# Wide mask matmuls ahead of the scores, and three early loads split by partitions, in an attention and SwiGLU kernel

## The chip, the cores and the metric

One core of one Trainium2 chip. The metric is the device time of the whole kernel in microseconds (us), lower is better. In traces, PE is TensorE, PEld its weight load, DVE VectorE, ACT ScalarE, POOL GpSimd, SP the engine that issues the DMAs.

## The reference

```python
def _attn_ref(q, k, v):                      # [8, 8, 576, 64], float32
    scores = q @ k.T / 8                     # per batch and head
    rel = pos[:, None] - pos[None, :]
    scores = where((rel >= 0) & (rel < 64), scores, -1e9)
    return softmax(scores) @ v
def _moe_ref(x, w_gate, w_val, w_out):       # x: [4608, 512], d_ff 1536
    g = x @ w_gate
    return (g * sigmoid(g) * (x @ w_val)) @ w_out
```

A causal sliding window of 64 keys, then a gated feed-forward block.

## The kernel before

Tokens go in 36 groups of 128. Queries, keys and values are loaded in float32, cast to bf16, turned by TensorE, and each group's scores, weights and products are worked between feed-forward steps. The first groups are masked in PSUM, by adding -1e30 through a matmul of a constant (`minus`) with the identity; later groups are masked after the exponential by VectorE. The parts that the change touches:

```python
    def load_vg(g):

        if g % 2 == 0:
            staged["v_f", g // 2] = stage.tile([P, 2, H, D], FP32, name="v_f", tag="v_f")[:]
        for y, b, s in tokens(g):
            m = y.stop - y.start
            sp.dma_start(
                staged["v_f", g // 2][y, g % 2],
                v[b, :, s:s + m, :].rearrange("h r d -> r h d"))
...
    def scores(g, masked=False):

        ps = [ps_a.tile([P, 4, 2, 64], FP32, name="s_ps", tag="a") for _ in range(2)]
        for b in range(2):
            o = P * (g % 2) + 64 * b
            for p in range(4):
                for a in range(2):
                    y = slice(64 * a, 64 * a + 64)
                    keys = kT[g // 2 % KR][y, p, o:o + P]
                    if ORDER[g][1] is None:
                        keys = kL[y, p, ORDER[g][0] + b, :]
                    nc.tensor.matmul(
                        ps[a][:, p, b], keys, qT[g // 2 % QR][y, p, o:o + 64],
                        tile_position=(64 * a, 0), start=True, stop=not masked,
                    )
                if masked:
                    for a in range(2):
                        y = slice(64 * a, 64 * a + 64)
                        m = minus[1 if ORDER[g][1] == 0 and b == 0 else 0]
                        nc.tensor.matmul(
                            ps[a][:, p, b], m[y], identb[y, y], tile_position=(64 * a, 0),
                            start=False, stop=True,
                        )
        sps[g] = ps, masked
...
    def weights(s, i):
        src = (moe_w_gate, moe_w_val)[i]
        w_f = wst.tile([P, 4, 256], FP32, name="w_f", tag="w_f")
        sp.dma_start(w_f[:], src[:, 256 * s:256 * s + 256].rearrange("(c r) f -> r c f", r=P))
        raw[i, s] = w_f
```

The schedule is written by hand; its start, in the order in which each engine gets its work (`warm(n)` is n matmuls on zeros whose result nothing uses):

```python
    begin()
    load(0, k, "k_f")
    load(0, q, "q_f")
    load(1, k, "k_f")
    load_vg(0)
    cast_k(0, "q_f", (dve, act))
    cast_k(0, "k_f", pool)
    warm(11)
    turn2(0, "k_f", (act, dve))
    load(1, q, "q_f")
    warm(3)
    turn2(0, "q_f", (act, dve))
    warm(3)
    scores(0, True)
    scores(1)
    load_vg(1)
    cast_k(1, "k_f", (act, dve))
    cast_v(0, (pool, act, dve))
    load_vg(2)
    load_vg(3)
    cast_v(1, pool)
    weigh(1)
    weights(5, 0)
    weigh(0)
    warm(7)
    turn2(1, "k_f", act)
...
```

Here `scores(0, True)` is a masked group; seven groups are (0, 2, 3, 5, 4, 7, 6). `weights(5, 0)` is the first slice of the gate weights: 128 rows of 4 pieces of 1 KB.

The softmax here doesn't subtract the row's maximum and nothing guards it: scores larger than these inputs give would overflow.

## Time and profile before

| | before |
|---|---|
| time, median | 338.14 us (337.61 to 338.68) |
| TensorE busy | 327.6 us, 97% |
| TensorE idle, 8 to 39 us of the span | 4.3 us |
| TensorE idle, 39 to 332 us | none |
| matmuls and weight loads on TensorE | 2825 + 2825 = 5650 (the prediction counts 5652) |

Two stages: up to about 38 us the DMA engines are full (share 1.06 from 8 to 40 us) and TensorE waits for data now and then; after that TensorE never waits. One thing is needed to follow the rest: each load of 128 rows in this kernel, and each of the later ones of 64 rows, leaves 16 landing records in the trace. They are read here as one from each of the core's 16 DMA engines, though no record names its engine, and a load is taken as there when the last one is. Landings below are read from these records; where a view shows them indirectly, it is as the start of the cast that waits for the load.

### The profile page before, as it was taken

Reading aid. Unit: us, or ns where it says so; the run is one execution under the profiler, and the core shown is the slowest. Engines: PE = TensorE matmul, PEld = TensorE weight load, DVE = VectorE, ACT = ScalarE, POOL = GpSimd, SP = SyncE. Lnnn points to the kernel's source line nnn. Section 1 sums busy time; section 2 is a strip of 40 time slices with the busy share of each in tenths; the row PEclk is TensorE's granted clock in tenths of the full one; section 3 lists DMA queues with packets and bytes.
Section 4 is the critical chain, followed back from the end, with each engine's and each line's share of the span. In section 5 each row is a group of like instructions: output and inputs, shape, how many; then the busy total and the mean of one; then the engine's idle time right before and its main releaser. Section 6 shows DMA issues by size and latency. Waiting matters only on the chain.

```text
span 336.9 us, 7388 instructions
## 1 busy us (share of the span) xinstructions
PE 327.6 (97%) x2825; PEld 164.1 (49%) x2825; DVE 226.3 (67%) x491; ACT 151.9 (45%) x268; POOL 100.5 (30%) x148
## 2 busy tenths in 40 slices
PE   7898999999999999999999999999999999999996
PEld 3555665555544444444444444444444444444444
DVE  4657889895676666666676767766667766655520
ACT  3766876664634343434343443434343434233222
POOL 4444356660053333333333333223333200000000
DMA  8999999998978999798879798999787720211013
GB/s 209 247 312 264 280 301 326 322 185 194 228 137 149 192 151 190 151 193 162 181 151 194 137 195 174 158 179 181 158 180 157 104 62 34 65 31 31 33 47 109
DMA packets 150612, 56.85 MB, mean 169 GB/s; under 512 B 124721, under 2 KB 144561, under 8 KB 150577
## 3 DMA queue, kind: packets, MB, share of 16 engines
q1 hardware_dynamic: 150576, 56.38, 77.5%
q8 instruction: 22, 0.36, 0.5%
q14 instruction: 14, 0.11, 0.2%
HBM read 37.75 MB, written 9.44 MB: 140 GB/s over the span
## 4 chain that ended last, share of the span: by engine, by line
PE 87%; DMA 8%; SPq 3%; ACT 1%; POOL 0%; issue 0%; ACTq 0%; POOLq 0%
PE g_ps L309 27%; PE o_ps L327 27%; PE v_ps L309 26%; DMA q_f<-in_q_dram 6%; PE ao_ps L245 3%; PE s_ps L207 3%; DMA v_f<-in_v_dram 2%; SPq L110 1%; SPq L89 1%; PE tp L170 1%; DMA out_dram<-os__4994 1%; PE xtp L269 0%; POOL q_fb L120 0%; ACT q_fb L118 0%; ACT os__4994 L332 0%
## 5 line engine op out<-in xcount | busy, mean ns | idle before, releaser
L309 PE MATMUL g_ps<-xT,wg 128*128 128x512 bf16 (+1 forms) x460 | 112.4, 367 | 0.2
L309 PE MATMUL v_ps<-xT,wv 128*128 128x512 bf16 (+1 forms) x460 | 112.1, 366 | 0.5 <-ACT wv L118 0.5
L320 DVE SCALAR_TENSOR_TENSOR sg<-th,g_ps 128x512 f32<-128x512 f32 (+1 forms) x115 | 75.0, 652 | 53.8 <-ACT th L314 53.5
L314 ACT ACTIVATE th<-g_ps 128x512 f32<-128x512 f32 (+1 forms) x115 | 65.9, 573 | 76.4 <-PE g_ps L309 73.6
L327 PE MATMUL o_ps<-wo,hT 128*128 128x512 bf16 (+2 forms) x456 | 98.5, 368 | 0.0
L321 DVE TENSOR_TENSOR hT<-sg,v_ps 128x512 bf16<-128x512 f32 (+1 forms) x115 | 75.4, 656 | 11.9 <-PE xtp L269 0.5
L309 PEld LDWEIGHTS <-wv 128*128 128x128 bf16 x460 | 44.7, 98 | 49.4 <-ACT wv L118 1.0
L327 PEld LDWEIGHTS <-hT 128*128 128x128 bf16 x456 | 43.6, 98 | 49.5
L309 PEld LDWEIGHTS <-wg 128*128 128x128 bf16 x460 | 41.8, 98 | 42.3 <-issue 0.6
L227 ACT ACTIVATE E<-s_ps 128x512 bf16<-128x512 f32 x72 | 38.5, 596 | 8.0 <-PE s_ps L207 8.0
L120 POOL CAST q_fb<-q_f 128x1024 bf16<-128x1024 f32 x13 | 13.6, 1044 | 64.9 <-DMA q_f<-in_q_dram 41.2
L120 POOL CAST k_fb<-k_f 128x1024 bf16<-128x1024 f32 (+1 forms) x16 | 16.0, 1003 | 56.1 <-DMA k_f<-in_k_dram 46.1
L256 DVE TENSOR_TENSOR x_b<-ao_ps,r 128x256 bf16<-128x256 f32 x72 | 30.6, 425 | 2.5
L120 POOL CAST ve<-v_f 64x512 bf16<-64x512 f32 x47 | 28.9, 615 | 2.9
L229 DVE TENSOR_TENSOR E<-E,mask 128x512 bf16<-128x512 bf16 x58 | 23.3, 427 | 9.1 <-ACT E L227 8.3
L120 POOL CAST vo<-v_f 128x512 bf16<-128x512 f32 x30 | 18.9, 630 | 30.3 <-DMA v_f<-in_v_dram 30.1
L255 DVE RECIPROCAL r<-ao_ps 128x4 f32<-128x4 f32 x72 | 12.6, 174 | 5.4 <-PE ao_ps L245 5.3
L245 PEld LDWEIGHTS <-E 128*64 128x64 bf16 x576 | 11.0, 110 | 7.8 <-issue 5.7
L207 PEld LDWEIGHTS <-kT 64*128 64x128 bf16 x512 | 10.1, 95 | 6.6 <-issue 4.0
L120 POOL CAST vL<-v_f 64x512 bf16<-64x512 f32 x15 | 9.6, 638 | 10.2 <-DMA v_f<-in_v_dram 9.5
L207 PE MATMUL s_ps<-qT,kT 64*128 64x64 bf16 x512 | 12.2, 191 | 0.4 <-DVE x_b L256 0.3
L245 PE MATMUL ao_ps<-ve,E 128*64 128x65 bf16 x256 | 11.9, 196 | 0.1
(100 smaller groups left out, 150.1 us busy)
## 6 DMA issues: line engine op xcount, KB each, us to landing
v_f<-in_v_dram SPq DMA_DIRECT2D x32, 256.0 KB, 4.6
k_f<-in_k_dram SPq DMA_DIRECT2D x20, 256.0 KB, 4.1
q_f<-in_q_dram SPq DMA_DIRECT2D x18, 256.0 KB, 4.7
q_f<-in_q_dram SPq DMA_DIRECT2D x7, 512.0 KB, 7.0
k_f<-in_k_dram SPq DMA_DIRECT2D x6, 512.0 KB, 7.6
w_f<-in_moe_w_gate_dram SPq DMA_DIRECT2D x6, 512.0 KB, 6.2
w_f<-in_moe_w_val_dram SPq DMA_DIRECT2D x6, 512.0 KB, 6.5
wo_f<-in_moe_w_out_dram SPq DMA_DIRECT2D x6, 512.0 KB, 7.3
```

Source lines behind the costliest of these rows:

```text
L120: eng.tensor_copy(y, x)
L207: nc.tensor.matmul(ps[a][:, p, b], keys, qT[g // 2 % QR][y, p, o:o + 64], tile_position=(64 * a, 0), start=True, stop=not masked,)
L227: act.activation(e, x[:], AF.Exp, scale=0.125)
L229: dve.tensor_mul(e, e, mk[:].unsqueeze(1).to_broadcast([P, 4, 2, 64]))
L245: nc.tensor.matmul(o_ps[64 * b:64 * b + 64, i, :], Es[g % ER][:, y, b], z[:, y, :], tile_position=(0, 64 * b),)
L255: dve.reciprocal(r[:], o_ps[:, :, D])
L256: dve.tensor_mul(xb[g][:, 256 * h:256 * h + 256].rearrange("r (y d) -> r y d", y=4), o_ps[:, :, 0:D], r[:].unsqueeze(2).to_broadcast([P, 4 ...
L309: nc.tensor.matmul(ps[:, 0:n], w[:, c, P * m:P * m + P], xT[t][:, c, c0:c0 + n], start=(c == 0), stop=(c == 3),)
L314: act.activation(th[:, 0:n], g_ps[:, 0:n], AF.Tanh, scale=0.5)
L320: dve.scalar_tensor_tensor(sg[:, 0:n], th[:, 0:n], 1.0, g_ps[:, 0:n], ALU.add, ALU.mult)
L321: dve.tensor_mul(hT[t][:, m, c0:c0 + n], sg[:, 0:n], v_ps[:, 0:n])
L327: nc.tensor.matmul(o_ps[:, a:b], hT[t][:, c, P * s:P * s + P], wo[:, c, a:b], start=(c == 0), stop=(c == 11),)
```

## The change

Intent: (1) mask a whole PSUM tile by one wide matmul per row half, ahead of the scores, in place of one narrow matmul after each score: 18 mask matmuls in place of 112. (2) Split three early loads by partitions, so that some DMA engines get less of them.

```diff
--- before.py
+++ after.py
@@ -101,15 +101,17 @@
                 sp.dma_start(x_f[y, i], src[b, :, s:s + m, :].rearrange("h r d -> r h d"))
         staged[nm, n] = x_f[:]
 
-    def load_vg(g):
+    def load_vg(g, cut=P):
 
         if g % 2 == 0:
             staged["v_f", g // 2] = stage.tile([P, 2, H, D], FP32, name="v_f", tag="v_f")[:]
         for y, b, s in tokens(g):
             m = y.stop - y.start
-            sp.dma_start(
-                staged["v_f", g // 2][y, g % 2],
-                v[b, :, s:s + m, :].rearrange("h r d -> r h d"))
+            for i, j in ((0, min(m, cut)), (cut, m)):
+                if i < j:
+                    sp.dma_start(
+                        staged["v_f", g // 2][y.start + i:y.start + j, g % 2],
+                        v[b, :, s + i:s + j, :].rearrange("h r d -> r h d"))
 
     words = {}
 
@@ -196,6 +198,20 @@
     def scores(g, masked=False):
 
         ps = [ps_a.tile([P, 4, 2, 64], FP32, name="s_ps", tag="a") for _ in range(2)]
+        if masked:
+
+            first = ORDER[g][1] == 0
+            for b in range(2 if first else 1):
+                for a in range(2):
+                    y = slice(64 * a, 64 * a + 64)
+                    z, n = ps[a][:].rearrange("r p b x -> r (p b) x"), 8
+                    if first:
+                        z, n = ps[a][:, :, b], 4
+                    nc.tensor.matmul(
+                        z, minus[1 if first and b == 0 else 0][y],
+                        identb[y, y].unsqueeze(1).to_broadcast([64, n, 64]),
+                        tile_position=(64 * a, 0), start=(b == 0), stop=False,
+                    )
         for b in range(2):
             o = P * (g % 2) + 64 * b
             for p in range(4):
@@ -206,16 +222,9 @@
                         keys = kL[y, p, ORDER[g][0] + b, :]
                     nc.tensor.matmul(
                         ps[a][:, p, b], keys, qT[g // 2 % QR][y, p, o:o + 64],
-                        tile_position=(64 * a, 0), start=True, stop=not masked,
+                        tile_position=(64 * a, 0), start=not masked,
+                        stop=not masked or (b == 1 and p == 3),
                     )
-                if masked:
-                    for a in range(2):
-                        y = slice(64 * a, 64 * a + 64)
-                        m = minus[1 if ORDER[g][1] == 0 and b == 0 else 0]
-                        nc.tensor.matmul(
-                            ps[a][:, p, b], m[y], identb[y, y], tile_position=(64 * a, 0),
-                            start=False, stop=True,
-                        )
         sps[g] = ps, masked
 
     def weigh(g):
@@ -278,10 +287,13 @@
 
     raw = {}
 
-    def weights(s, i):
+    def weights(s, i, cut=P):
         src = (moe_w_gate, moe_w_val)[i]
         w_f = wst.tile([P, 4, 256], FP32, name="w_f", tag="w_f")
-        sp.dma_start(w_f[:], src[:, 256 * s:256 * s + 256].rearrange("(c r) f -> r c f", r=P))
+        x = src[:, 256 * s:256 * s + 256].rearrange("(c r) f -> r c f", r=P)
+        for y in (slice(0, cut), slice(cut, P)):
+            if y.start < y.stop:
+                sp.dma_start(w_f[y], x[y])
         raw[i, s] = w_f
 
     def cast_w(s, i, eng):
@@ -394,11 +406,11 @@
     load_vg(1)
     cast_k(1, "k_f", (act, dve))
     cast_v(0, (pool, act, dve))
-    load_vg(2)
-    load_vg(3)
+    load_vg(2, 120)
+    load_vg(3, 104)
     cast_v(1, pool)
     weigh(1)
-    weights(5, 0)
+    weights(5, 0, 100)
     weigh(0)
     warm(7)
     turn2(1, "k_f", act)
```

## The prediction

> **What bounds the kernel now.** I read the page's busy shares first, then the slices, then the chain that ended last in order of time, then the waits of TensorE, and last the DMA records around the loads that the change touches.
>
> ```profile
> PE 327.6 (97%) x2825; PEld 164.1 (49%) x2825; DVE 226.3 (67%) x491; ACT 151.9 (45%) x268; POOL 100.5 (30%) x148
> ...
> PE   7898999999999999999999999999999999999996
> ...
> DMA  8999999998978999798879798999787720211013
> ```
>
> TensorE (PE) is busy 97% of the span; the only slices short of 9 are the first few. DMA is at 8 or 9 tenths over the same start. So there are two stages. Asked for busy time by stage (columns: stretch, its length, busy us and count by engine, clock, DMA share, GB/s), the trace says so sharply:
>
> ```profile
> 8.00:40.00 32.00, 27.70 (x455) 17.45 (x455) 22.60 (x57) 23.69 (x44) 14.19 (x19) 1.00 1.06 273
> 40.00:76.00 36.00, 36.00 (x394) 20.61 (x387) 32.71 (x71) 24.55 (x43) 21.11 (x28) 1.00 1.08 284
> 76.00:320.00 244.00, 244.00 (x1875) 116.00 (x1874) 166.09 (x344) 97.27 (x172) 61.07 (x86) 1.00 0.73 143
> ```
>
> From 40 us on TensorE is busy 36.00 of 36.00 and 244.00 of 244.00 us: whatever is to be won there must be matmul time itself. From 8 to 40 us it idles 4.3 us, and the DMA engines are full (share 1.06; over 1 because packets of one engine overlap). The chain that ended last, in order of time (start, length, what), tells which transfers carry the start:
>
> ```profile
> 9.61 6.56 DMA v_f<-in_v_dram
> ...
> 16.52 10.66 DMA q_f<-in_q_dram
> ...
> 28.16 8.91 DMA q_f<-in_q_dram
> ...
> 37.20 1.05 POOL q_fb L120
> 38.25 0.04 issue
> 38.30 0.62 PE tp L170 x8
> 38.91 0.44 PE g_ps L309 x4
> ```
>
> Three loads, then a cast, then the transposes at 38.30; after that only TensorE to 331.90 and the last store. The end is therefore (the moment at which the queries of block 3 are turned, about 38.3) plus 293.6 us of dense TensorE work plus some 5 us. TensorE's own waits between 10 and 39 us:
>
> ```profile
> PE tp L170 <- DVE q_fb L120: 1.0, 1, 1.0
> PE tp L170 <- ACT q_fb L118: 0.9, 1, 0.9
> PE xtp L269 <- ACT E L227: 0.6, 1, 0.6
> PE v_ps L309 <- ACT wv L118: 0.5, 1, 0.5
> PE tp L170 <- DVE k_fb L120: 0.4, 1, 0.4
> PE s_ps L207 <- DVE x_b L256: 0.3, 1, 0.3
> PE tp L170 <- POOL k_fb L120: 0.2, 1, 0.2
> ```
>
> They sum to 3.9 us; the idle time of the trace from 8 to 39 us is 4.3 us. That is the ceiling of anything that only brings data sooner.
>
> Two more records matter. The masks:
>
> ```profile
> L215 PE MATMUL s_ps<-identb,minus x112: 188/190/200, 8.6 to 40.6; 64*128 64x64 bf16 x112
> ```
>
> [...] in the timeline the pairs (two row halves) start 0.03 us apart. And a 16 KB instruction fetch runs on the DMA engines just when the loads in question are in flight, as the DMA view of 11.5 to 13.5 us shows (packets, MB, share):
>
> ```profile
> q8 instruction: 1, 0.02, 4.1%
> ```
>
> Its packet starts at 11.97 us and takes 1.31 us; the next such fetches are at 21.98 and 33.19 us, and one of 8 KB is at 28.54 us (1.32 us). [...] The load of values 2, issued at 8.38 us, has 15 landings by 13.9 us and the last at 15.2; values 3, issued at 9.61, has 15 by 14.9 and the last at 16.2; the first weight slice 16.9 and 17.6. After the fetch at 21.98 the keys of block 2 land 23.9 and 25.4, their queries 25.7 and 27.2. After those at 28.54 and 33.19 the queries of block 3 have 14 landings by 35.6 and the last two at 36.8 and 37.1. So one DMA engine, held up by a fetch, delays each following load by 1.2 to 1.5 us, and the sequencer that issues (its queue full all through this stage) waits with it.
>
> [...] 4 matmuls of 512 columns take 0.86 us, pairs of 64 columns start 29 ns apart. [...] two halves together take those 29 ns. [...]
>
> **The change part by part.** (1) Masks. Seven score groups are masked (0, 2, 3, 5, 4, 7, 6). Removed: 7 x 16 = 112 matmuls of 64 columns with as many weight loads. Added: 2 groups that start a sequence x 4 of 256 columns, and 5 x 2 of 512: 18 matmuls. Cost before, per group: 8 pairs x 29 ns = 0.232 us. After: one pair of 512, 0.216 us, or two pairs of 256, 2 x 0.109 = 0.218 us. The columns are the same; [...] about 0.015 us a group, 0.1 us in all. Only groups 7 and 6 (39.7 to 40.7 us) lie in the dense stage: 0.03 us of certain gain. (2) The instruction stream of TensorE is shorter by 2 x 94 = 188 (5652 to 5464), 24 less in group 0 and 28 in each of 2, 3, 5. Over the run 22 fetches for some 5652 instructions is about 257 each, so 188 is three quarters of a fetch, all in the first 41 us. By counting, the first fetch moves from 11.97 to about 13.2 us (24 instructions on), the second from 21.98 to about 28 (80 on, as TensorE waits there), the third from 33.2 to about 36. The keys and queries of block 2 would then not meet the second fetch. (3) The splits. Values 2: 120 rows on 15 engines and 8 on 8; values 3: 104 on 13 and 24 on 12; the weight slice: 100 on 10 and 28 on 14. [...] A 256 B packet takes 18 ns and a 1 KB one 46 ns in the trace, so a value row is 8 x 18 = 0.15 us and a weight row 4 x 46 = 0.18: [...] plus 0.45 + 0.74 = 1.2 us for the most loaded. If the engine of the fetch is the last one, values 2 land at about 13.9 + 0.15 = 14.1 in place of 15.2, values 3 at about 15.2 in place of 16.2. ScalarE casts them 1 us sooner, and its exponentials of groups 2 and 3 follow, worth most of the 0.6 us wait of the transposes and part of the 0.3. The weight slice stays near 17.6: 12 rows in place of 8 on ten engines. Three more issues of some 0.5 us (the shortest in the trace) fall in a queue that is full anyway, so they are hidden.
>
> The sum: 0.5 us in the waits to 18 us; the keys and queries of block 2 at max(23.9 + 1.2, no straggler) = 25.1 and 26.9 by load alone, up to 1 us better as the queue no longer stalls on one engine, so 0.4 to 1.0 of the 1.5 us of waits at 26 to 28; the last wait of 0.6 us before 38.3 partly, as the second late engine at 36.8 may remain. These add to 0.9 to 1.9 us of the 4.3; [...] I take 1.2 us.
>
> **Rivals.** (a) Nothing: [...] the straggler becomes later by up to 1.2 us and every load of the start with it; the time is 338.5 to 339.5. For it: no record names the engine. [...] (b) The start gains, but TensorE is held at 38.3 by the queries of block 3, whose arrival is bandwidth, not lag: bytes are unchanged and the load is now uneven. Then the gain is under 0.4 us, 337.8. For it: DMA share 1.06 in that stage. (c) The wide masks run their halves one after the other, as no 512-column pair exists before: 0.216 more in each group, of which two are on the path, +0.4 us. Against it: the 64-column pairs overlap fully. (d) All waits of the start melt: minus 3 us, 335. It needs every load sooner, and the 0.95 us at 11.7 is upstream of the change.
>
> **Range and chances.** 338.14 - 1.2 = 336.9. The two runs before differ by 1.07 us, so half a microsecond is noise; with (a) and (c) above and (d) below, 335.5 to 338.5 should hold it 8 times in 10. Two per cent is 6.8 us, more than all idle time from 8 us on, so faster by that is at 0.01; slower by that would need the whole start to slip by 6.8 us: 0.01; within, 0.98.
>
> **What would show it.** Right: landings of values 2 and 3 near 14 and 15 us; ScalarE's casts of them about 1 us earlier; instruction fetches later by the counts above and one fewer; the wait of the transposes on the query cast near 27 us shorter; TensorE without idle time after some 37 us; the two masked groups near 40 us still some 0.9 us together. Wrong: the last landing of the three loads no sooner, the queries of block 3 still at 37 us, or wide masks whose halves start 0.2 us apart.

The sum came to 0.9 to 1.9 us: 0.5 in the waits to 18 us, 0.4 to 1.0 around block 2, and up to 0.4 left for the last wait of 0.6. Its author took 1.2 of it, 338.14 - 1.2 = 336.9, after a deduction. The "last one" of the engines was assumed to get nothing of the cut parts. The "most loaded" one was taken to get three value rows (0.45) and four weight rows (0.74) more. The number of engines of each part is borne out by the trace of the changed kernel: parts of 120, 8, 104, 24, 100 and 28 rows leave 15, 8, 13, 12, 10 and 14 landings. The 0.109 us of a 256-column matmul and the 0.216 of a 512-column one are the distances of their starts in the trace before. The queue that issues is full in that the issues from 0.8 to 39 us follow each other with gaps of at most 0.2 us. That the scores add to a mask put in first rests on the results, which were correct.

## The result, and the profile after

The changed kernel takes 340.37 us (340.16 to 340.57) where 335.5 to 338.5 was predicted: 2.2 us slower where 1.2 us of gain was expected. All outputs are right. The ratio is 1.0070, 95% interval 1.0046 to 1.0093. A ratio here is the mean time of one kernel's fast runs over that of the other's fast runs of the same rounds, so it is not quite the ratio of the medians quoted beside it. Later, with more rounds, the same kernel gave 1.0041 (1.0013 to 1.0068).

The page of the changed kernel (busy totals; TensorE's busy tenths in 40 slices), to be held against the first fence of the prediction:

```profile
PE 328.0 (97%) x2731; PEld 163.9 (48%) x2731; DVE 226.7 (67%) x491; ACT 151.9 (45%) x268; POOL 101.2 (30%) x148
...
PE   7877999999999999999999999999999999999996
```

TensorE's busy total is 0.4 us more, and the loss is in the first slices. The stretches show the same (same columns as in the prediction):

```profile
8.00:40.00 32.00, 26.17 (x362) 15.98 (x360) 21.05 (x56) 22.75 (x42) 13.07 (x17) 1.00 1.08 255
40.00:76.00 36.00, 36.00 (x381) 20.99 (x380) 32.16 (x71) 25.49 (x45) 20.71 (x27) 1.00 1.13 296
```

From 8 to 40 us TensorE is busy 26.17 us in place of 27.70, so it idles 1.5 us more; from 40 to 76 us it is full as before. Its waits between 10 and 39 us:

```profile
PE tp L172 <- ACT q_fb L120: 1.6, 1, 1.6
PE g_ps L321 <- POOL wg L122: 1.1, 1, 1.1
PE tp L172 <- DVE q_fb L122: 1.0, 1, 1.0
PE v_ps L321 <- POOL wv L122: 0.6, 1, 0.6
PE g_ps L321 <- DVE sg L332: 0.5, 1, 0.5
PE xtp L278 <- ACT E L236: 0.5, 1, 0.5
```

New are the waits for GpSimd's casts of weights (`wg` 1.1, `wv` 0.6) and for VectorE's `sg` that follows; the wait for the queries of block 2 (ScalarE, `q_fb`) grew from 0.9 to 1.6. The wait of the transposes for the exponentials (`xtp`) shrank only from 0.6 to 0.5. The chain that ended last (start, length, what):

```profile
11.73 4.74 DMA v_f<-in_v_dram
...
18.51 11.10 DMA q_f<-in_q_dram
...
29.63 0.63 ACT q_fb L120
...
40.19 0.45 PE tp L172 x8
```

The queries of block 3 are turned at 40.19 us by this view, where before it was 38.30. That is the result in one line. By the start times of TensorE's matmuls in the trace the turn starts 1.72 us later (40.02 against 38.30), the stretch from there to the first output projection takes 34.34 us against 34.38, and the last part 261.66 against 261.16: 1.72 - 0.04 + 0.50 = 2.18 us, the difference of the two ends of TensorE's work (336.02 and 333.84). Of the 1.72 us, 0.44 stand in this profile ahead of anything that the change touches: TensorE's first wait for keys ends at 6.57 us in place of 6.12, and the wait for the queries of block 1 at 13.09 in place of 12.65. In the repeat of the change told below the latter ends at 12.64 us and the turn is at 39.71, so some 1.4 us of the lateness at the turn go with the change.

What came late are the weight slices. GpSimd's casts of the first three, before (start, length, operation, idle before and what ended it):

```profile
17.65 1.04 POOL L120 CAST wg<-w_f 128x1024 bf16<-128x1024 f32 x1 [0.28 <-DMA w_f<-in_moe_w_gate_dram]
19.18 1.04 POOL L120 CAST wv<-w_f 128x1024 bf16<-128x1024 f32 x1 [0.49 <-DMA w_f<-in_moe_w_val_dram]
20.75 1.04 POOL L120 CAST wg<-w_f 128x1024 bf16<-128x1024 f32 x1 [0.52 <-DMA w_f<-in_moe_w_gate_dram]
```

and after:

```profile
20.94 1.04 POOL L122 CAST wg<-w_f 128x1024 bf16<-128x1024 f32 x1 [3.42 <-DMA w_f<-in_moe_w_gate_dram]
22.15 1.04 POOL L122 CAST wv<-w_f 128x1024 bf16<-128x1024 f32 x1 [0.17 <-DMA w_f<-in_moe_w_val_dram]
23.65 1.04 POOL L122 CAST wg<-w_f 128x1024 bf16<-128x1024 f32 x1 [0.46 <-DMA w_f<-in_moe_w_gate_dram]
```

The first slice is cast 3.3 us later and the next two 3.0 and 2.9 us later. In landings: the first slice is complete at 20.8 us in place of 17.6.

### The profile page after: what moved, and what is told of

It is laid out like the page before. It is cut to its first block, busy times and chain, and to the rows that moved or that the text cites. A ratio compares the mean times of both kernels' runs of the same rounds, so it can differ in the third digit from the quotient of the medians.

```text
span 338.9 us, 7208 instructions
## 1 busy us (share of the span) xinstructions
PE 328.0 (97%) x2731; PEld 163.9 (48%) x2731; DVE 226.7 (67%) x491; ACT 151.9 (45%) x268; POOL 101.2 (30%) x148
## 4 chain that ended last, share of the span: by engine, by line
PE 84%; DMA 6%; SPq 4%; ACT 2%; DVE 2%; issue 1%; ACTq 0%; DVEq 0%
PE g_ps L321 26%; PE o_ps L339 26%; PE v_ps L321 25%; DMA q_f<-in_q_dram 3%; PE ao_ps L254 3%; PE s_ps L223 2%; SPq L112 2%; DMA v_f<-in_v_dram 1%; SPq L89 1%; PE tp L172 1%; DMA kT<-k_fb 1%; ACT E L236 1%; DMA out_dram<-os__4903 1%; DVE sg L332 1%; PE xtp L278 1%
## 5 line engine op out<-in xcount | busy, mean ns | idle before, releaser
L238 DVE TENSOR_TENSOR E<-E,mask 128x512 bf16<-128x512 bf16 x58 | 24.6, 452 | 9.3 <-ACT E L236 8.7
L352 PE MATMUL w_ps<-wz 128*128 128x512 bf16 x33 | 10.8, 464 | 1.3 <-DVE wz L356 1.3
L254 PE MATMUL ao_ps<-vo,E 128*64 128x65 bf16 x256 | 11.9, 196 | 0.0
```

Source lines behind the costliest of these rows:

```text
L238: dve.tensor_mul(e, e, mk[:].unsqueeze(1).to_broadcast([P, 4, 2, 64]))
L254: nc.tensor.matmul(o_ps[64 * b:64 * b + 64, i, :], Es[g % ER][:, y, b], z[:, y, :], tile_position=(0, 64 * b),)
L352: nc.tensor.matmul(w_ps[:], wz[:, 0:P], wz[:])
```

## The experiments

Each kernel ran with a profile and five timed rounds beside the kernel before. The times are medians of six runs; the kernel before had a median of 338.6 to 338.7 in every job; the jobs ran on three chips.

| kernel | time, us | ratio to before | 95% interval |
|---|---|---|---|
| the change again | 339.95 | 1.0041 | 1.0013 to 1.0068 |
| masks alone | 337.68 | 0.9977 | 0.9959 to 0.9996 |
| all splits alone | 339.84 | 1.0038 | 1.0017 to 1.0059 |
| slice split alone | 339.20 | 1.0022 | 1.0000 to 1.0043 |
| all three split at 64 | 338.88 | 1.0018 | 0.9995 to 1.0041 |
| masks + slice split | 339.11 | 1.0018 | 0.9998 to 1.0038 |
| masks + value splits | 338.61 | 0.9998 | 0.9980 to 1.0015 |
| wide masks in group 0 only | 337.39 | 0.9967 | 0.9949 to 0.9985 |
| wide masks but group 0 | 339.58 | 1.0041 | 1.0008 to 1.0074 |
| masks + slice at 96 | 338.66 | 1.0001 | 0.9973 to 1.0029 |
| masks + slice at 120 | 339.21 | 1.0021 | 0.9995 to 1.0048 |
| masks + slice by chunks | 337.60 | 0.9972 | 0.9947 to 0.9996 |
| masks + slice in halves | 338.84 | 1.0010 | 0.9985 to 1.0036 |
| masks + slice odd/even | 337.97 | 0.9985 | 0.9960 to 1.0009 |
| group 0 wide, padded | 338.06 | 0.9987 | 0.9955 to 1.0019 |

### Which part: masks alone, splits alone

Edit for the masks alone (against the change):

```diff
-    load_vg(2, 120)
-    load_vg(3, 104)
+    load_vg(2)
+    load_vg(3)
-    weights(5, 0, 100)
+    weights(5, 0)
```

For the splits alone, `scores` is the function before.

> The wide masks as in the change, no load split. Theory A (uneven rows: ten DMA engines get 12 rows of the weight slice in place of 8, so everything behind it lands late): no part of the loss is here; within 0.5 us of before, at best 1 us faster, as the second instruction fetch moves away from the keys and queries of block 2. Rival B (the shorter TensorE stream moves a fetch, seen at 16.0 us in place of 12.0, onto worse loads): 1 to 2 us slower than before, with a straggler in the landings of the weight slices.

> The three splits as in the change, masks as before. Theory A: all of the loss, 1.5 to 2.5 us slower than before, the value slice of the weights landing near 22 us in place of 19. Rival B: within 0.5 us of before.

The twelve rows in place of eight on ten engines are an estimate from landings of the changed kernel: 100 rows on 10 landings and 28 on 14, where 128 were on 16. Of the 14, four come by 17.2 us and ten from 19.0 to 20.8; of the next slice, six by 19.5 and ten from 20.8 to 22.1.

The masks alone gain 0.8 us (ratio 0.9977); the splits alone lose 1.3. Rival B falls. Theory A had the sign, but it placed the loss of the splits in late weight slices (the value slice lands at 20.9 us, not near 22), and in this pair the trace shows another wait ahead of it, TensorE's longest between 10 and 39 us with the splits alone:

```profile
PE xtp L271 <- ACT E L229: 2.0, 1, 2.0
```

It was 0.6 us before. The exponentials wait behind ScalarE's cast of values 3, whose last landing came at 17.5 us in place of 16.2: later, not sooner. The value splits need not be what made it late. With the slice split alone, told below, the values are loaded whole, and their last landing is at 17.8 us and the same wait is longer:

```profile
PE xtp L271 <- ACT E L229: 2.3, 1, 2.3
```

So with narrow masks the slice split is enough for this wait; the value splits with narrow masks were not run by themselves. Why the slice split delays a load issued ahead of it, no run shows.

The landings of the splits alone tell why the value splits did not help. The packet of the first instruction fetch starts at 12.00 us and takes 1.4 us. The 120-row part of values 2 has one straggler (15.9, all others by 14.2); the 8-row part has none (all by 14.5); the 104-row part has one (16.9, others by 15.6), the 24-row part too (17.5, others by 15.9), the 100-row part of the slice none (18.1 to 19.1). The parts of 120, 8, 104, 24, 100 and 28 rows leave 15, 8, 13, 12, 10 and 14 landings here, each with one more record at the end of the issue. If a landing is an engine, and the straggler the one that the fetch held, then the held engine had a share of the 120, the 104 and the 24 rows. The value splits do not relieve it; by the counts the split of values 3 gives it 8 + 2 rows in place of 8, an estimate. Which engine it is, and whether it is the same in every kernel, is not shown. In the slice split alone the ten landings of the 100-row part come by 18.5 us, too soon after 17.8 for ten more rows (1.8 us at 0.18, an estimate), so the straggler of values 3 seems not to be among them; in the repeat of the change, told below, a straggler is.

The page of the splits alone also has a line for TensorE's granted clock, in tenths:

```profile
PEclk9979999999999999999999999999999999999999
```

After that wait of 2.0 us the clock record has a half-rate stretch of 3.41 us from 18.97 us on, which the kernel before had not. The profiles of the slice split alone, the even splits, and the masks with the slice split have one too (from 18.94, 19.29 and 23.06 us, after waits of 2.3, 1.7 and 1.5 us). What it adds to the loss of such runs was not isolated: of the timed runs some have a granted clock of 0.99 to 0.995 and others of 0.999 or 1.00. The loss of the change does not hang on it: neither of its profiles has such a stretch in the start, though TensorE's longest wait in each between 10 and 39 us is 1.6 us, so the length of the wait does not decide alone; and five of the six runs of its repeat are at 1.00, with a mean of 339.86 us.

### The weight slice, and whether issues cost

Edits: only `weights(5, 0, 100)` kept, with the narrow masks; and, for the even splits, 64 in place of 120, 104 and 100.

> Only the weight slice split at 100, masks and values as before. Theory A: most of the loss, 1.0 to 2.0 us slower than before, as 4 rows of 0.18 us more on ten engines delay all that follows; landings of the next slices in two groups, six engines ahead of ten by some 1.5 us. Rival C (three more issues and their semaphore waits cost, not the rows): a third of the loss, 0.7 us.

> The same three loads split at 64 rows, so both parts run on 16 engines with 4 rows each; masks as before. Theory A: within 0.5 us of before, since no engine has more rows. Rival C (three more issues): the same 1.5 to 2.5 us slower as the splits of the change.

The slice split alone loses 0.7 us (1.0022, the interval touches 1), under the expected 1.0 to 2.0; the even splits lose 0.6 us with an interval that holds 1. Rival C falls: it asked for 1.5 to 2.5 us, and the interval of the even splits ends at 1.4. Theory A is not confirmed either: it asked for more from the slice split, and with the even splits the transposes still wait 1.7 us for the exponentials, though no engine has more rows (loads of 64 rows leave 16 landings in the traces before and after; its profile is the slowest of its six runs). That was the first hint that "rows per engine" is not the whole of it.

### The parts with the wide masks

> The change itself, to be timed in the same rounds as its parts (the masks alone gave 0.8 us of gain, the splits alone 1.2 us of loss, the whole 2.2 us of loss in another job). If the parts simply add, 0.4 us slower than before; if they work against each other, 1.5 to 2.5 us slower. Landing of the second weight slice about 22 us, a late instruction fetch at about 16 us.

> Wide masks and the weight slice split at 100, values whole. Theory A2 (with the masks the fetch comes at 16 us, when the slices are in flight, and the slice split leaves its engine and nine others 4 rows more): most of the loss, 1.0 to 2.0 us slower than before, the second slice landing at 21 us or later where the masks alone have 19.5. Rival: the value splits do it, and this one stays within 0.5 us of before.

> Wide masks and both value splits, the weight slice whole. Theory A2: within 0.6 us of before, a little slower than the masks alone (values 3 near 16 us in place of 15.2). Rival (the value splits do it): 1.0 to 2.0 us slower than before.

Against the masks alone (337.68), the slice split costs 1.43 us, the value splits 0.93, both together, which is the change, 2.27: with the wide masks the two splits add up. The change itself is at 1.0041, or 1.4 us slower than before, just under the range expected if the parts worked against each other and over the 0.4 us expected if they simply added. Masks alone plus splits alone make only +0.5 of its +1.4 (by the ratios, -0.8 and +1.3); as the three intervals are some 0.4 points wide, whether there is more than addition in it can't be said. Masks with the slice split, 0.6 us slower than before by the ratio, fall between their two expectations, though the second slice lands at 21.3 us as theory A2 said. Masks with the value splits came out within theory A2's range; there the value parts are slower (256 B packets of 28 ns in place of 25, from 12.0 to 13.8 us), and the slice, at 16.7 us with the masks alone, is in flight when the fetch comes at 15.79 and lands at 17.4 but for one straggler at 18.9. In the masks with the slice split, the ten engines of the 100-row part land at 17.7 to 18.1 us, where with the masks alone the whole slice is there at 16.7.

### Where the first instruction fetch falls

Edit: the narrow `scores` kept under another name, and called for six of the seven groups, or for group 0 alone.

> Wide masks in group 0 only, the other six masked groups as before, no splits: 24 instructions fewer ahead of the first fetch and 164 of the 188 kept. Theory F (the masks gain by moving the first fetch past the value loads): if the fetch moves to about 13 to 16 us, values 3 land at 15.2 in place of 16.2 and the gain of the masks, 0.3 to 1.0 us, is all here; if it stays at 12, no gain. Rival G (the gain is TensorE time or the length of the whole stream): within 0.2 us of before, wherever the fetch is.

> Wide masks in the six masked groups other than group 0, no splits: 164 of the 188 instructions go, but none ahead of the first fetch. Theory F (the gain of the masks is where the first fetch falls): fetch at 12 us as before, values 3 at 16.2, the transposes wait again, no gain: within 0.3 us of before. If the fetch moves nonetheless, the gain comes with it. Rival G (length of the stream or TensorE time): gain as with all masks wide, 0.8 us.

With wide masks in group 0 only, 24 instructions fewer, the first fetch starts at 15.84 us in place of 11.98, values 3 land at 15.2 in place of 16.2, and the kernel is at 0.9967, 1.1 us faster than before, the fastest measured (337.39; the masks alone at 337.68 are not distinguishable from it). With all but group 0 wide, the fetch stays at 12.09 and nothing is gained. Rival G falls. The trace shows what goes with a fetch at 12 us. Before, the issue of the first weight slice (start, length) is held:

```profile
11.37 2.34 SPq L284 DMA_DIRECT2D w_f<-in_moe_w_gate_dram  x1
```

and what the DMA engines move from 13.8 to 15.2 us is

```profile
DMA packets 443, 0.18 MB, mean 131 GB/s; under 512 B 346, under 2 KB 443, under 8 KB 443
```

With wide masks in group 0 only, the same issue and the same stretch:

```profile
11.34 1.03 SPq L321 DMA_DIRECT2D w_f<-in_moe_w_gate_dram  x1
```

```profile
DMA packets 623, 0.38 MB, mean 268 GB/s; under 512 B 337, under 2 KB 623, under 8 KB 623
```

The issuing queue is held for 2.34 us in place of 1.03, and the engines as a whole, not only the fetched-on one, move less: 131 against 268 GB/s. That hole of 1.4 us at half the rate is about 0.7 us of transfer, and the later loads of the start come about that much sooner without it (15 of the 16 landings of the keys of block 2 by 23.0 us in place of 23.9). With all but group 0 wide the issue is held as before (2.37 us). A fetch at 12 us does not always do it: in the slice split alone it starts at 11.84 us and the issue of the slice's first part, at 11.21, takes 1.10. The prediction saw the late engine, but not the hole.

That the other variant is slower than before by 0.4% was not expected. Its turn of block 3 is at 38.35 us, as before (38.30); the loss of 1.18 us in its profile is later, 0.49 us up to the first projection and 0.64 after it. More on that below.

The padding puts 24 instructions back ahead of the fetch:

```diff
+        for _ in range(small):
+            nc.tensor.matmul(w_ps[:, 0:8], wz[:, 0:P], wz[:, 0:8])
...
-    warm(7)
+    warm(7, 12)
```

> Wide masks in group 0 alone, and 12 matmuls of 8 columns on zeros (24 instructions) put after the idle-time matmuls ahead of the first fetch, where TensorE waits anyway; results untouched. Theory F (the place of the fetch): the fetch is back at 12 us, values 3 land at 16.2, and the time is back at before, 0.8 to 1.5 us slower than without the padding. Rival (the wide masks of group 0 gain by themselves): the time stays near 337.4, 1 us faster than before, wherever the fetch is.

This one is inconclusive. The fetch came back to 12.99 us, not 12.0; values 3 land at 16.5 as expected of the theory, yet the issue of the slice is done by then (1.03 us) and there is no hole (276 GB/s in the same stretch), and the profiled execution is as fast as without padding (span 335.4 us against 335.6). The straggler is back and the transposes wait 0.9 us for it, so in this profile a late engine alone costs nothing in the end; that fits the hole as the cost, but it is argued from one profile. Of the six timed runs three took 336.9 to 337.4 and three 338.8 to 339.4, and what parts them on record is TensorE's granted clock: 1.00 in the first three, 0.995 in the others. Half a per cent of 337 us is 1.7 us, of the 2.0 us between their means. By that estimate a lower clock makes most of the difference without any hole, and the median of this variant says nothing on the place of the fetch.

### Why the split slice is slow

Edits: the slice split at 96 or at 120 rows; or along its free dimension, all rows in each part:

```diff
-        for y in (slice(0, cut), slice(cut, P)):
-            if y.start < y.stop:
-                sp.dma_start(w_f[y], x[y])
+        for y in (slice(0, 2), slice(2, 4)) if cut < P else (slice(0, 4),):
+            sp.dma_start(w_f[:, y], x[:, y])
```

> Wide masks, weight slice split at 96 rows: by the landings seen so far that is 16 engines with 6 rows, then 16 with 2, so no engine has more work than before. Theory I (uneven rows alone delay the slices): 1 KB packets stay at a median of about 48 ns, the slice lands by 16.9 us, time as the masks alone, about 0.8 us faster than before. Theory P ([...] its packets take longer: 71 to 76 ns were seen with the split at 100): packets of 60 ns or more, slice 0.7 us or more later than 16.7, time 0.3 to 0.8 us worse than the masks alone.

> Wide masks, weight slice split at 120 rows: 15 engines with 8 rows, 8 engines with one row more. Theory I: 0.2 us later than 16.7 for the slice, time within 0.3 us of the masks alone. Theory P: packets of 60 ns or more and the slice at 17.4 us or later, time 0.3 to 1.0 us worse than the masks alone.

> Wide masks, weight slice split in two along its free dimension, each part with all 128 rows: one issue more, as with the splits by rows, but the rows of each engine as before. Theories I and P: packets of 48 ns, slice by 16.9 us, time as the masks alone within 0.3 us. Rival C (the extra issue costs): 0.5 us or more worse than the masks alone.

What the DMA engines moved from 15.3 to 16.2 us, while the slice is in flight, with the masks alone:

```profile
DMA packets 313, 0.32 MB, mean 355 GB/s; under 512 B 16, under 2 KB 312, under 8 KB 312
```

with the slice at 96, at 120, and by chunks:

```profile
DMA packets 225, 0.23 MB, mean 253 GB/s; under 512 B 18, under 2 KB 224, under 8 KB 224
```

```profile
DMA packets 206, 0.21 MB, mean 233 GB/s; under 512 B 1, under 2 KB 206, under 8 KB 206
```

```profile
DMA packets 317, 0.32 MB, mean 358 GB/s; under 512 B 17, under 2 KB 316, under 8 KB 316
```

At 96 rows no engine has more rows than before (16 landings for each part), and still the rate is 253 in place of 355 GB/s, and the median 1 KB packet takes 72 ns in place of 51. At 120 it is 233 GB/s and 80 ns. By chunks, with one issue more but all 128 rows in each, nothing is lost (358 GB/s, 51 ns, 337.60 us). So the extra issue is free, and the slice in two parts of consecutive rows is slow here whether its engines are evenly filled (96 and 32 rows) or not (120 and 8). The time of the kernel at 96 (interval 0.9973 to 1.0029) does not by itself prove a loss against the masks alone; the rates do.

Is it that a part has fewer than 128 rows, or which rows it has? The last pair tests that: contiguous halves against odd and even rows (`slice(0, P, 2), slice(1, P, 2)`), with the same rows per engine, packet sizes and issues. The author expected the contiguous halves to be slow and the others not.

> Wide masks, weight slice split at 64: rows 0 to 63, then 64 to 127, 4 rows per engine each. [...] the first half runs well under 340 GB/s, packets of 1 KB above 60 ns; the time 0.3 to 1.0 us worse than the masks alone. Rival (any load of fewer than 128 rows is slow): the same.

> Wide masks, weight slice split into even and odd rows, 4 rows per engine each. [...] packets near 50 to 60 ns and the slice at 16.9 us or sooner, the time within 0.4 us of the masks alone. Rival (any load of fewer than 128 rows is slow): as the contiguous halves.

Halves, then odd and even, in the same stretch:

```profile
DMA packets 197, 0.19 MB, mean 209 GB/s; under 512 B 13, under 2 KB 197, under 8 KB 197
```

```profile
DMA packets 316, 0.32 MB, mean 352 GB/s; under 512 B 22, under 2 KB 315, under 8 KB 315
```

209 against 352 GB/s, 80 against 49 ns a packet. The rival (any load of fewer than 128 rows is slow) falls: 64 rows at a time run at 352 GB/s when they are every second row, beside 355 for the whole slice. In time the halves are at 338.84 and the interleaved rows at 337.97, with intervals that overlap. (The first part of the interleaved slice is there at 16.0 us and 15 of the 16 landings of the second at 16.7; the last, at 18.2, is behind the fetch at 15.36.) So it matters which rows a part has; why consecutive ones are slow, no run shows. For 96, 100 and 120 rows the slow rate is measured, without an interleaved counterpart.

### A late wait of the shorter stream

The stretch from the first output projection to the end takes 261.16 us in all five kernels with an instruction stream of the old length (before, splits alone, slice split alone, even splits, padded group 0), and 261.34 to 262.39 in the twelve profiles of a shorter one. In the profiles looked at closely a wait of 0.4 to 0.6 us stands behind a burst of score matmuls near 260 us, put down to VectorE's `sg`; a fetch had begun 3 to 4 us earlier. That the shifted fetches cause it is likely, not shown.

## Why the prediction was wrong, point by point

**What bounds the kernel.** Right: the end is the turn of block 3 plus dense work. The turn moved by 1.72 us and the end by 2.18.

**The masks on TensorE.** Right. The two groups on the path, after the change:

```profile
41.44 0.39 PE L210 MATMUL s_ps<-identb,minus 64*128 64x512 bf16 x2
41.66 0.40 PE L223 MATMUL s_ps<-qT,kT 64*128 64x64 bf16 x16
41.90 0.38 PE L210 MATMUL s_ps<-identb,minus 64*128 64x512 bf16 x2
42.11 0.40 PE L223 MATMUL s_ps<-qT,kT 64*128 64x64 bf16 x16
42.44 0.61 PE L321 MATMUL g_ps<-xT,wg 128*128 128x256 bf16 x4
```

41.44 to 42.44 us is 1.00 us for both, where they took 39.72 to 40.76, 1.04: 0.04 us of gain for a predicted 0.03. A pair of 512 columns is followed by the scores 0.22 us later, so the halves run together, and rival (c) falls.

**The fetches.** Right in direction and in number (21 for 22), wrong in size (16 KB fetches are counted; in the first 45 us of both profiles their packets take 1.1 to 1.4 us each): "By counting, the first fetch moves from 11.97 to about 13.2 us" was 16.04 in the first profile and 14.86 in the second, the second fetch at 26.3 to 26.6 for "about 28". Counting instructions does not give the place of a fetch. What can go with a fetch was also left out: not only a late engine, but half the rate in all of them together (131 in place of 268 GB/s) where the issuing queue is held (2.34 us in place of 1.03).

**"If the engine of the fetch is the last one."** This step failed twice. Where the fetch comes at 12 us, with the splits alone, there is a straggler in the 120-row, the 104-row and the 24-row part (15.9, 16.9 and 17.5 us), so the value splits did not relieve it. With the masks the fetch comes later (16.0 and 14.9 us), and no value part has a straggler left to relieve (values 2 and 3 are complete at 14.6 and 16.2 us in the repeat, for a predicted 14.1 and 15.2); the fetch meets the slice, and in the repeat of the change its straggler is among the ten engines of the 100-row part (20.6 us, eight others by 18.9), which by the landings had been given four rows more (10 + 2 in place of 8, an estimate). Rival (a), a straggler that becomes later, named this case; at 338.5 to 339.5 it was still short of the 340.0 to 340.4 measured.

**"A weight row 4 x 46 = 0.18."** The mis-sized term. Four rows more were to cost ten engines 0.74 us, and "the weight slice stays near 17.6". In the repeat most of them land at 18.7 to 18.9 for the 100-row part and 19.5 to 19.9 for the rest, and the last at 21.0; with the masks alone the slice is there at 16.7. The median 1 KB packet there took 71 to 81 ns in the three profiles with wide masks and the slice split at 100, in place of 46 to 51. The row's price was read from loads of 128 rows and does not hold for this split. That a split alone can do this, and that it hangs on which rows a part has, is shown for halves (209 GB/s for contiguous rows, 352 for every second one); for the split at 100 only the slow packets are measured. The value splits cost 0.9 us beside the masks, in place of gaining 0.5. Their row was too cheap as well: a 256 B packet has a median of 18 ns over the whole run, but of 24 while values 2 and 3 load (12.0 to 13.8 us), and of 27 to 28 there with the cut values and the wide masks.

**Three more issues are hidden.** Right, as far as one extra issue by chunks shows (0.9972 against 0.9977 for the masks alone).

**"They add to 0.9 to 1.9 us; I take 1.2."** The masks do bring 0.8 us, group 0 alone 1.1, so nearly all of the hoped-for sum was there, in the part of the change to which the sum gave the least; the splits took 2.3 us away.

## What to carry to other kernels

Before a load is cut by partitions to relieve a DMA engine, ask what the cut does to the rate of each part: a cut along the free dimension, or into odd and even rows, kept 350 GB/s here where contiguous rows fell to 210 to 250. In a start that is bound by transfers, a few instructions more or fewer ahead of an instruction fetch can be worth a microsecond, so look for the fetch packets in the DMA records and for what the issuing queue does then; and try such a part alone, since here one part gained 0.8 to 1.1 us and the other hid it. Look at the granted clock of every timed run before explaining two groups of times: in the padded variant it parts them.
